# A recurrence and a token-mixing layer in one kernel: the same 1169 steps in another written order, with a fixed place for every tile

## The chip, the cores and the metric

The kernel runs on one core of one Trainium2 chip. The metric is the time of one execution on the device in microseconds (us); lower is better. A core has TensorE (PE, matmuls; its weight loads are shown apart as PEld), VectorE (DVE), ScalarE (ACT), GpSimd (POOL) and SyncE (SP, which issues the DMAs here). Each engine works through its own list of instructions strictly in order and waits on semaphores for the others.

## What is computed

The reference has two parts. The first is a gated linear recurrence over 768 positions for 4 batches of 8 heads of 48 values; its output is the input `x` of the second, a mixing layer:

```python
f = 1.0 / (1.0 + np.exp(-f_logit))
for t in range(S):
    state = f[:, :, t, :, None] * state + np.einsum('bhd,bhe->bhde', k[:, :, t], v[:, :, t])
    y[:, :, t] = np.einsum('bhd,bhde->bhe', q[:, :, t], state)
...
theta = x @ w_theta
zr, zi = x * np.cos(theta), x * np.sin(theta)
y = np.einsum('ts,bsd->btd', w_tok_r, zr) + np.einsum('ts,bsd->btd', w_tok_i, zi)
u = x + y
return u + np.maximum(u @ w_ch, 0.0)
```

The weights are 64-bit floats, which the kernel reads as pairs of 32-bit words and turns into 32-bit values on the chip.

## The kernel before

The 768 positions of a batch are six chunks of 128, so 24 chunks `m` in all. One function issues each step of the work for one chunk, one part of the weights or one group of outputs. The whole program is the table `ORDER`: 35 strings of two-letter step names. The loop at the end of the table's code calls the function of each name in turn, the n-th time for the n-th chunk, part or group. All five engines are under a manual schedule, so this one list fixes the order in which every engine does its instructions, the DMAs on SP's queue included. A suffix (`/A`, `/D`, `/P`) sets `here[0]`, and steps that ask for it (`on(...)`) go to ACT, DVE or POOL. Steps that name their engine ignore it.

The steps, by name:

- `lf lk lq lv lw` load the gates, keys, queries, values and one part of the weights.
- `gc go gs ge gp gq gk` clamp the gate's logits, take the log of the gate (ACT), sum it along the chunk (a scan on DVE), take both exponentials (ACT), keep the last column (POOL), and scale the queries and keys (`gk` is on DVE).
- `ke kt` transpose a chunk's keys on PE (tile `psk`) and copy them out (`ktok`). `sc` makes the scores (PE, `sk`), `up` the sums of the state (PE, also `sk`), `ma` masks the scores (DVE, `sc`). `sa st sm` update the state (`mid`, `st`). `qs` and `ou` make the chunk's output on PE (`py`), and `xc xt xs` copy it out (`x`), transpose it (PE, `pxt`) and keep it (`ut`).
- `th` multiplies by `w_theta` (PE, `pth`); `tn se ab tr` reduce the angle and take sine and cosine (DVE, ACT); `ro` multiplies by `x` (always on DVE); `zh zl` and `xh xl` split into a high and a low part.
- `d1 d2 d3 di d4 d5` decode and split the weights (`d2` is always on ACT).
- `f0 f1 f2` are the products with the token weights for one third of the channels (PE, `pm`); `v` adds them to `ut` (DVE); `uh ul` split the sum; `c` is the product with `w_ch` (PE, `pch`); `cv` finishes (DVE) and `so` stores.
- `fl` and `rv` find out whether a gate was too small for this way of computing. The branch that recomputes everything in that case is not taken here.

Batch 0 multiplies 32-bit values without a split (`pm<-value`, `pth<-value`); the other three use the split parts (`pm<-wp`). PE has three kinds of matmul: those with 128x128 weights and 384 columns; transposes with 128x128 weights and 128 columns; and the small ones of `sc up qs ou`, whose weights stand in 64 rows.

Tiles come from pools by a tag with a number of buffers, taken in turn: four PSUM banks `b`, two PSUM pairs `a`, six tiles `z`, 25 `wp`, three each of `f k q v x`. A tile waits for the last reader of the one that had its buffer before.

Of the kernel before, what the change touches and what calls it, by code (L numbers as in the profile page):

```python
# [49 lines left out]

ORDER = (
# [35 lines left out]
)  # L89


# [1 line left out]
def gla_moe_kernel(  # L93
# [16 lines left out]
    sb = ctx.enter_context(tc.tile_pool(name="sb", bufs=1))  # L110
    dram = ctx.enter_context(tc.tile_pool(name="dram", bufs=1, space=bass.MemoryType.DRAM))
    ps = ctx.enter_context(tc.tile_pool(name="ps", bufs=1, space=bass.MemoryType.PSUM))

    xt_d = dram.tile([B, DM, S], F32, tag="xt_d", name="xt_d")

# [465 lines left out]
    def recurrence(b):  # L581
# [6 lines left out]
        for p in range(NP):  # L588
# [3 lines left out]
                nc.sync.dma_start(t.rearrange("r (c t) -> r c t", c=NC), src[b, :, :, p, :].rearrange("c r t -> r c t"))  # L592
            nc.sync.dma_start(vr, vt[b, p])
            nc.scalar.activation(fr, fr, AF.Sigmoid)
            acc = [ps.tile([P, TH], F32, tag="b", bufs=4, name=f"acc{p}{h}") for h in range(NTH)]
            for e in range(D):

                sel = sb.tile([P, 2, 64], F32, tag="w", bufs=2, name=f"sel{p}{e}")
                for j in range(2):
                    nc.vector.tensor_copy(sel[:, j, :], ident[:, 64 * j + e:64 * j + e + 1].to_broadcast([P, 64]))  # L600
                kv = kvs[e % 2]
                for h in range(NTH):
                    hs = slice(h * TH, (h + 1) * TH)
                    bc = bank([P, TH], f"bc{p}{e}{h}")
                    nc.tensor.matmul(bc, sel.rearrange("p j m -> p (j m)"), vr[:, hs], start=True, stop=True)
                    nc.vector.tensor_tensor(kv[:, hs], kr[:, hs], bc, op=ALU.mult)
                nc.vector.tensor_tensor_scan(st, fr, kv, 0.0, ALU.mult, ALU.add)
                nc.vector.tensor_tensor(kv, qr, st, op=ALU.mult)
                for h in range(NTH):
                    nc.tensor.matmul(acc[h], pick[:, 47 - e:47 - e + P], kv[:, h * TH:(h + 1) * TH],  # L610
                                     start=(e == 0), stop=(e == D - 1))
# [5 lines left out]
    with tc.If(over[0] > 0, preferred_fallthrough_block=False):  # L617
        with tc.For_i(0, B, 1) as b:
            recurrence(b)
            for m in range(NC):  # L620
                if m == 0:
                    uts[0] = u_tile("r")
                uts[1] = uts[LAST]
                nc.sync.dma_start(u_slice(m), xt_d[b, :, m * C:(m + 1) * C].rearrange("(k p) t -> p k t", p=P))
                px = bank([P, DM], f"rpx{m}")
# [73 lines left out]
```

## Time and profile before

| | |
|---|---|
| median of 3 runs | 339.72 us (339.62 to 339.76) |
| the profiled execution's own time | 340.03 us |
| its span, from the first to the last instruction | 338.3 us |
| PE busy | 320.4 us, 95% of the span |
| DVE, ACT, POOL busy | 251.6, 188.7, 108.6 us |
| DMA | 45.54 MB |

The profiled execution took 1.73 us more than its span, and 0.31 us more than the median. "Busy" for PE is modelled from pipelined matmuls, so 95% doesn't say that 95% of PE's time was well used. Where PE is read closely, the starts of its instructions and the reasons for its waits count.

### The profile page before, as it was taken

What the parts mean: (1) busy time and instruction counts of PE and PEld (TensorE: products, weight loads), DVE (VectorE), ACT (ScalarE), POOL (GpSimd) and SP (SyncE); (2) the same over time, 40 slices, a digit from 0 to 9 for tenths busy, and PEclk for the clock granted to TensorE, in tenths of its full rate; (3) what the DMA queues carried; (4) which work ended last, traced back from release to release, by engine and by line L of the source; (5) the groups of instructions that cost most, each with busy time, mean ns of one, the idle gap of its engine ahead of it and who ended that gap; (6) DMA issues with size and microseconds to landing.
All of it is one profiled execution on the core that took longest, in us unless ns stands there. A gap on an engine that the chain in (4) does not pass through costs nothing. (4 is left out here: it accounts for less than half of the span.)

```text
span 338.3 us, 9998 instructions
## 1 busy us (share of the span) xinstructions
PE 320.4 (95%) x4320; PEld 283.2 (84%) x4320; DVE 251.6 (74%) x411; ACT 188.7 (56%) x308; POOL 108.6 (32%) x105
## 2 busy tenths in 40 slices
PE   0789999999999999999999999999999999999993
PEld 0676766776776789999999999999999999999992
DVE  5989999999999998898987857855437848534211
ACT  6787997995866755588476685244076114400010
POOL 3585152134418235701445423323212201300010
PEclk9999999999999999999999999999999999999998
DMA  7994994738761262374124320532121120000012
GB/s 256 382 401 168 317 372 151 249 114 323 244 224 30 64 230 82 91 233 141 33 85 149 122 79 2 187 114 84 40 73 48 47 73 27 0 2 0 11 60 78
DMA packets 21618, 45.54 MB, mean 135 GB/s; under 512 B 2368, under 2 KB 5440, under 8 KB 21568
## 3 DMA queue, kind: packets, MB, share of 16 engines
q1 hardware_dynamic: 21568, 44.84, 38.5%
q8 instruction: 36, 0.59, 0.7%
q14 instruction: 14, 0.11, 0.1%
HBM read 40.11 MB, written 4.72 MB: 133 GB/s over the span
## 5 line engine op out<-in xcount | busy, mean ns | idle before, releaser
L458 PE MATMUL pm<-wp,z 128*128 128x384 f32 x648 | 118.4, 337 | 0.0
L458 PEld LDWEIGHTS pm<-wp,z 128*128 128x128 f32 x648 | 112.4, 188 | 0.4
L458 PE MATMUL pm<-value,z 128*128 128x384 f32 x144 | 49.3, 487 | 0.0
L476 PE MATMUL pch<-uhl,wch 128*128 128x384 f32 x216 | 40.0, 337 | 0.0
L458 PEld LDWEIGHTS pm<-value,z 128*128 128x128 f32 x144 | 26.4, 190 | 15.2
L476 PEld LDWEIGHTS pch<-uhl,wch 128*128 128x128 f32 x216 | 37.4, 188 | 0.0
L469 POOL TENSOR_TENSOR uhl<-ut,uhl 128x384 fp32r<-128x384 f32 x13 | 14.2, 1094 | 67.0 <-ACT uhl L143 35.5
L236 POOL TENSOR_SCALAR f<-f 128x512 f32<-128x512 f32 x16 | 26.6, 1666 | 13.3 <-DMA f<-in_f_dram 12.5
L246 DVE TENSOR_TENSOR_SCAN f<-carry,f 128x512 f32<-128x512 f32 x24 | 29.8, 1246 | 1.4 <-ACT f L242 1.4
L257 POOL COPY pes<-p 128x4 f32<-128x4 f32 x24 | 10.5, 439 | 52.9 <-ACT p L253 52.9
L490 DVE SCALAR_TENSOR_TENSOR ut<-pch,ut 128x384 f32<-128x384 f32 x24 | 13.1, 550 | 18.8 <-PE pch L476 17.1
L308 PE MATMUL psk<-ident,k 128*128 128x128 f32 x96 | 16.9, 303 | 10.0 <-DVE k L266 10.0
L261 POOL TENSOR_TENSOR q<-q,p 128x512 f32<-128x512 f32 x12 | 17.3, 1446 | 23.1 <-ACT p L253 14.6
L462 DVE TENSOR_TENSOR ut<-pm,ut 128x384 f32<-128x384 f32 x24 | 13.0, 551 | 14.2 <-PE pm L458 14.2
L253 ACT ACTIVATE p<-f 128x512 f32<-128x512 f32 x24 | 15.1, 630 | 14.4 <-DVE f L246 6.8
L402 PE MATMUL pth<-wth,xh 128*128 128x384 f32 x108 | 23.0, 348 | 0.0
L308 PEld LDWEIGHTS psk<-ident,k 128*128 128x128 f32 x96 | 12.2, 153 | 12.3 <-issue 10.3
L435 DVE TENSOR_TENSOR w<-w,x 128x768 f32<-128x768 f32 x18 | 17.2, 962 | 6.3 <-ACT w L426 6.3
L143 ACT COPY x<-py 128x384 f32<-128x384 f32 x19 | 9.1, 478 | 22.5 <-PE py L361 22.1
L361 PEld LDWEIGHTS py<-v,sc 64*64 64x64 f32 x768 | 15.0, 140 | 7.4 <-issue 4.5
L143 ACT CAST uhl<-ut 128x384 fp32r<-128x384 f32 x7 | 3.6, 513 | 31.1 <-DVE ut L462 17.5
L266 DVE SCALAR_TENSOR_TENSOR k<-f,k 128x512 f32<-128x512 f32 x24 | 18.2, 758 | 1.8 <-ACT f L254 1.1
(83 smaller groups left out, 622.6 us busy)
## 6 DMA issues: line engine op xcount, KB each, us to landing
v<-in_v_dram SPq DMA_DIRECT2D x24, 384.0 KB, 4.3
f<-in_f_dram SPq DMA_DIRECT2D x24, 256.0 KB, 3.8
q<-in_q_dram SPq DMA_DIRECT2D x24, 256.0 KB, 4.1
k<-in_k_dram SPq DMA_DIRECT2D x24, 256.0 KB, 4.3
raw<-in_w_r_dram SPq DMA_DIRECT2D x12, 384.0 KB, 5.9
raw<-in_w_i_dram SPq DMA_DIRECT2D x12, 384.0 KB, 6.3
out_dram<-ut SPq DMA_DIRECT2D x21, 192.0 KB, 1.9
raw<-in_w_theta_dram SPq DMA_DIRECT2D x3, 384.0 KB, 6.4
```

Source lines behind the costliest of these rows:

```text
L236: on(nc.vector).tensor_scalar(ft, ft, F_MIN, None, op0=ALU.max)
L246: nc.vector.tensor_tensor_scan(fl, carry[:, pairs(h)].rearrange("p n t -> p (n t)"), fl, 0.0, ALU.mult, ALU.add)
L253: nc.scalar.activation(ps_[m][:, pairs(h)], ft, AF.Exp, scale=-1.0)
L261: on(nc.vector).tensor_tensor(qt, qt, ps_[m][:, pairs(h)], op=ALU.mult)
L266: nc.vector.scalar_tensor_tensor(kt, loaded["f", m][:, pairs(h)], E_TOP, kt, op0=ALU.min, op1=ALU.mult)
L308: nc.tensor.transpose(psks[m][:, p, :], loaded["k", m][:, p, :], ident)
L361: nc.tensor.matmul(out[HALF[t], j, p, :], scs[m][HALF[a], j, p, :], v2[HALF[a], t, p, :], start=(t == 0 and m % NC == 0 and p == 0), stop= ...
L402: nc.tensor.matmul(pths[m], l, r, start=(n == 0), stop=(n == len(ms) - 1))
L435: nc.vector.tensor_tensor(zs[m] if full else w, w, xs[m].unsqueeze(1).to_broadcast([P, 2, DM]), op=ALU.mult)
L458: nc.tensor.matmul(pms[g, d], l, r, start=(s == 0 and i == 0), stop=(s == NC - 1 and i == len(ms) - 1))
L469: on(nc.vector).tensor_tensor(us[g, d][:, 0], uts[g][:, d, :], us[g, d][:, 1], op=ALU.subtract)
L476: nc.tensor.matmul(pcs[g, d], l, r, start=(es[0] == 0 and n == 0), stop=(es[-1] == KD - 1 and n == len(ms) - 1))
```

## The change

The counts of all steps stay. `ORDER` is replaced as a whole. The suffixes change with it: clamps on POOL 16 to 18, scalings of queries on POOL 12 to 18, casts of `uh` on DVE 17 to 7, on ACT 7 to 17, and some others by one to six. The new table also writes `ro/P` 14 times and `d2/P` 8 times, and these two steps name their engines in the code. A table `PLACES` gives each tile its buffer by a digit. The pools are wrapped so that each buffer is a tag of its own. Its strings for `f k q v x w sd uhl` are plain rotations, as before; those for the banks `a` and `b`, for `z` and for the end of `wp` are not.

```diff
+PLACES = {
+    "a": "0110101100110101010101010101010101010101010101010",
...
 ORDER = (
-    "lf gc lf gc go go gs lf gc/P lq lk lv gs ge gq gp go ge gk lw lk gs ke kt up gp sc lq gq/P d1 lw lq d2 gk ke",
...
+    "lf lf gc gc go go lf gc/P gs lk ge gp lq gq/P lw gs gk ke d1 lv lk lq lf go sc ge kt/D up lk gs gk gp sa st",
...
+    class Placed:
+        def __init__(self, pool):
+            self.pool, self.made = pool, {}
+
+        def tile(self, shape, dtype, tag=None, bufs=1, name=None, place=None):
+            n = self.made[tag] = self.made.get(tag, -1) + 1
+            own = PLACES.get(tag, "")
+            if place is None:
+                place = int(own[n], 36) if n < len(own) else n % bufs
+            return self.pool.tile(shape, dtype, tag=f"{tag}{place}", bufs=1, name=name)
+
+    sb, ps = Placed(sb), Placed(ps)
```

Three places show how instructions move. A name's first number is the chunk or part (`psk3` is of chunk 3), and the line numbers of the changed kernel are 31 higher for the same code.

PE before, around the first product with `w_theta` (`pth0`), from the state sums of chunk 2 on:

```order
L322 MATMUL sk1_291<-v2_214,ktok2_250 64x48 x16
L371 MATMUL pxt0_361<-ident_70,x0_277 128x128 x3
L361 MATMUL py1_310<-v1_205,sc1_367 64x48 x16
L308 MATMUL psk3_398<-ident_70,k3_252 128x128 x4
L353 MATMUL py2_411<-st1_275,q2_180 64x48 x2
...
L402 MATMUL pth0_436<-value0_176,ut0_365 128x384 x2
L402 MATMUL pth0_436<-value1_198,ut0_365 128x384
L297 MATMUL sk2_446<-q2_180,k2_209 64x64 x16
L322 MATMUL sk2_446<-v3_396,ktok3_403 64x48 x16
L371 MATMUL pxt1_479<-ident_70,x1_405 128x128 x3
```

PE of the change, from the same state sums on:

```order
L353 MATMUL sk1_282<-v2_210,ktok2_276 64x48 x16
L384 MATMUL py1_326<-st0_184,q1_132 64x48 x2
...
L402 MATMUL pxt0_348<-ident_70,x0_317 128x128 x3
L339 MATMUL psk3_354<-ident_70,k3_244 128x128 x4
L433 MATMUL pth0_377<-value0_126,ut0_369 128x384 x2
L433 MATMUL pth0_377<-value1_271,ut0_369 128x384
L392 MATMUL py1_326<-v1_186,sc1_382 64x48 x16
L384 MATMUL py2_415<-st1_278,q2_190 64x48 x2
...
L328 MATMUL sk2_437<-q2_190,k2_177 64x64 x16
L353 MATMUL sk2_437<-v3_400,ktok3_404 64x48 x16
L402 MATMUL pxt1_474<-ident_70,x1_408 128x128 x3
```

The output products of chunk 1 (`ou`, `py1<-v1,sc1`) and the queries against the state of chunk 2 (`qs`, `py2`) stood ahead of `pth0` and now stand behind it; `qs` of chunk 1 has gone behind the state sums of chunk 2.

DVE before, up to the mask of chunk 2 (`sc2`):

```order
L303 TENSOR_TENSOR sc1_367<-sk1_291,causal_75 128x512
L334 TENSOR_TENSOR st2_369<-sk1_291,mid2_359 128x192
L192 SCALAR_TENSOR_TENSOR raw2_279<-raw2_279 128x768
L193 SCALAR_TENSOR_TENSOR value2_355<-raw2_279 128x768
L246 SCALAR_TENSOR_TENSOR f4_241<-carry_67,f4_241 128x512
L217 TENSOR_TENSOR wth0_84<-value0_176,wth1_85 128x768
L182 TENSOR_SCALAR raw3_343<-raw3_343 128x768
L182 TENSOR_SCALAR raw4_347<-raw4_347 128x768
L338 TENSOR_TENSOR st2_369<-st2_369,pes_83 128x192
L246 SCALAR_TENSOR_TENSOR f5_308<-carry_67,f5_308 128x512
L266 SCALAR_TENSOR_TENSOR k4_352<-f4_241,k4_352 128x512
L303 TENSOR_TENSOR sc2_485<-sk2_446,causal_75 128x512
```

DVE of the change, up to the same mask:

```order
L361 TENSOR_TENSOR mid2_362<-sk1_282,st1_278 128x192
L174 COPY ut0_369<-pxt0_348 128x3x128
L365 TENSOR_TENSOR st2_371<-sk1_282,mid2_362 128x192
L277 SCALAR_TENSOR_TENSOR f4_196<-carry_67,f4_196 128x512
L277 SCALAR_TENSOR_TENSOR f5_251<-carry_67,f5_251 128x512
L334 TENSOR_TENSOR sc1_382<-sk1_282,causal_75 128x512
L213 TENSOR_SCALAR raw2_273<-raw2_273 128x768
L297 SCALAR_TENSOR_TENSOR k4_352<-f4_196,k4_352 128x512
L444 SCALAR_TENSOR_TENSOR w0_406<-w0_406,pth0_377 128x384
L174 CAST wth1_85<-value0_126 128x768
L213 TENSOR_SCALAR raw3_412<-raw3_412 128x768
L334 TENSOR_TENSOR sc2_492<-sk2_437,causal_75 128x512
```

The copy of chunk 0 out of its transpose (`ut0`) has come from ACT to DVE, the mask of chunk 1 (`sc1`) has gone behind two scans, and the decoding of weight part 2 (`value2`) has gone behind the mask of chunk 2.

DVE at the end of the program before (group 7 is the last):

```order
L469 TENSOR_TENSOR uhl70_4212<-ut7_3935,uhl70_4212 128x384
L490 SCALAR_TENSOR_TENSOR ut6_3272<-pch60_4259,ut6_3272 128x384
L490 SCALAR_TENSOR_TENSOR ut6_3272<-pch61_4269,ut6_3272 128x384
L490 SCALAR_TENSOR_TENSOR ut6_3272<-pch62_4308,ut6_3272 128x384
L462 TENSOR_TENSOR ut7_3935<-pm72_4215,ut7_3935 128x384
L565 TENSOR_LOAD flag_88
```

DVE at the end of the changed program:

```order
L493 TENSOR_TENSOR ut7_3912<-pm72_4179,ut7_3912 128x384
L521 SCALAR_TENSOR_TENSOR ut6_3237<-pch60_4274,ut6_3237 128x384
L521 SCALAR_TENSOR_TENSOR ut6_3237<-pch61_4306,ut6_3237 128x384
L521 SCALAR_TENSOR_TENSOR ut6_3237<-pch62_4319,ut6_3237 128x384
L174 CAST uhl72_4332<-ut7_3912 128x384
L500 TENSOR_TENSOR uhl71_4330<-ut7_3912,uhl71_4330 128x384
L500 TENSOR_TENSOR uhl72_4332<-ut7_3912,uhl72_4332 128x384
L596 TENSOR_LOAD flag_88
```

A cast and two subtractions for the last group now stand on DVE behind the three finishing steps of group 6; before, they were on ACT and POOL.

## Rows read from the trace of the kernel before

**Rows 1.** The page's head and its first part: busy time, share, instructions.
```profile
span 338.3 us, 9998 instructions
...
PE 320.4 (95%) x4320; PEld 283.2 (84%) x4320; DVE 251.6 (74%) x411; ACT 188.7 (56%) x308; POOL 108.6 (32%) x105
```

**Rows 2.** PE's longest wait over the span: us in total, times, longest.
```profile
PE psk L308 <- DVE k L266: 10.0, 2, 9.6
```

**Rows 3.** Stretches: us, PE, PEld, DVE, ACT, POOL, granted clock, DMA, GB/s.
```profile
20.00:30.00 10.00, 8.64 (x132) 6.26 (x125) 8.99 (x14) 8.54 (x15) 4.82 (x6) 1.00 0.89 340
...
50.00:60.00 10.00, 9.92 (x181) 6.41 (x183) 9.93 (x17) 7.43 (x11) 2.61 (x4) 1.00 0.46 152
...
290.00:300.00 10.00, 10.00 (x59) 10.00 (x58) 5.87 (x8) 3.39 (x6) 1.52 (x2) 1.00 0.00 0
```

**Rows 4.** PE in order of time, 21 to 36 us: start, duration, operation.
```profile
21.70 1.10 PE L322 MATMUL sk<-v,ktok 64*64 64x48 f32 x31 [1.05 <-issue]
22.73 0.90 PE L371 MATMUL pxt<-ident,x 128*128 128x128 f32 x3
23.94 1.14 PE L361 MATMUL py<-v,sc 64*64 64x48 f32 x32 [0.30 <-DVE sc L303]
25.01 1.11 PE L308 MATMUL psk<-ident,k 128*128 128x128 f32 x4
26.05 0.35 PE L353 MATMUL py<-st,q 48*64 48x48 f32 x2
...
27.09 4.19 PE L402 MATMUL pth<-value,ut 128*128 128x384 f32 x6
31.20 0.69 PE L297 MATMUL sk<-q,k 48*64 48x64 f32 x32
31.72 0.63 PE L322 MATMUL sk<-v,ktok 64*64 64x48 f32 x32
...
34.54 2.20 PE L402 MATMUL pth<-value,ut 128*128 128x384 f32 x6
```

**Rows 5.** PE's weight loads (PEld) where groups change, and two matmul groups.
```profile
32.56 0.47 PEld L308 LDWEIGHTS psk<-ident,k 128*128 128x128 f32 x4
33.19 0.59 PEld L361 LDWEIGHTS py<-v,sc 64*64 64x64 f32 x32 [0.17 <-DVE sc L303]
...
38.08 1.59 PEld L402 LDWEIGHTS pth<-value,ut 128*128 128x128 f32 x6
40.21 0.59 PEld L361 LDWEIGHTS py<-v,sc 64*64 64x64 f32 x32 [0.55 <-DVE w L413]
...
52.44 1.46 PE L458 MATMUL pm<-value,z 128*128 128x384 f32 x4
...
56.01 2.74 PE L458 MATMUL pm<-value,z 128*128 128x384 f32 x8
...
133.85 1.08 PEld L458 LDWEIGHTS pm<-wp,z 128*128 128x128 f32 x6
135.19 0.59 PEld L361 LDWEIGHTS py<-v,sc 64*64 64x64 f32 x32 [0.25 <-issue]
```

**Rows 6.** DVE at the mask of chunk 2, and its group of copies.
```profile
32.42 0.69 DVE L303 TENSOR_TENSOR sc<-sk,causal 128x512 f32<-128x512 f32 x1 [0.48 <-PE sk L322]
...
L143 DVE COPY ut<-pxt 128x384 f32<-128x384 f32 x7 | 3.8, 548 | 1.4 <-PE pxt L371 1.4
```

**Rows 7.** DVE and the last DMA in order of time, near the end.
```profile
308.55 0.34 DVE L143 CAST uhl<-ut 128x384 fp32r<-128x384 f32 x1
...
318.53 0.55 DVE L469 TENSOR_TENSOR uhl<-ut,uhl 128x384 fp32r<-128x384 f32 x1
...
331.63 1.67 DVE L490 SCALAR_TENSOR_TENSOR ut<-pch,ut 128x384 f32<-128x384 f32 x3 [3.08 <-PE pch L476]
333.43 0.39 SPq L650 DMA_DIRECT2D out_dram<-ut  x1
```

**Rows 8.** One decoding instruction, 0 to 30 us: shortest, median, longest, in ns.
```profile
L182 DVE TENSOR_SCALAR raw<-raw x5: 537/554/957, 10.6 to 28.4; 128x768 int32<-128x768 int32 x4, 128x384 int32<-128x384 int32 x1
```

More of the change, by code (lines that the diff above doesn't have):

```diff
@@ L46 @@
 CUT = 0
-ORDER = (
[35 rows of a table removed]
+PLACES = {
+    "a": "0110101100110101010101010101010101010101010101010",
+    "b": ("012301230123120232033303032313203300021021002312020222222012312102022000230122012100102101"
+        "0031213213212302302323302132013"),
+    "f": "012012012012012012012012",
+    "k": "012012012012012012012012",
+    "q": "012012012012012012012012",
+    "sd": "010101010101010101010101",
+    "st": "01010101010101010101",
+    "uhl": "01230123012301230123012301",
+    "ut": "01201201",
+    "v": "012012012012012012012012",
+    "w": "010101010101010101010101",
+    "wp": "0123456789abcdefghijklmno012347569ab",
+    "x": "012012012012012012012012",
+    "z": "0123450123401340340352401352401352401",
+}
+ORDER = (
[36 rows of a table added]
 )
@@ L594, in recurrence @@
             nc.scalar.activation(fr, fr, AF.Sigmoid)
-            acc = [ps.tile([P, TH], F32, tag="b", bufs=4, name=f"acc{p}{h}") for h in range(NTH)]
+            acc = [ps.tile([P, TH], F32, tag="b", bufs=4, name=f"acc{p}{h}", place=h) for h in range(NTH)]
             for e in range(D):
@@ L603, in recurrence @@
                     hs = slice(h * TH, (h + 1) * TH)
-                    bc = bank([P, TH], f"bc{p}{e}{h}")
+                    bc = ps.tile([P, TH], F32, tag="b", bufs=4, name=f"bc{p}{e}{h}", place=2 + h)
                     nc.tensor.matmul(bc, sel.rearrange("p j m -> p (j m)"), vr[:, hs], start=True, stop=True)
@@ L621, in gla_moe_kernel @@
                 if m == 0:
-                    uts[0] = u_tile("r")
+                    uts[0] = sb.tile([P, KD, TH], F32, tag="ut", bufs=3, name="utr", place=(int(PLACES["ut"][-1]) + 1) % 3)
                 uts[1] = uts[LAST]
```

69 rows, old and new, of the table ORDER are left out of this document.

## The prediction

> **What bounds the kernel now.** I read the page first, then PE's waits, the stretches, and PE's own rows in order of time. PE is busy for 320.4 of 338.3 us [rows 1]. Its only large wait is the one before its first matmul, 9.6 us, for the first scaled keys from DVE [rows 2]. After that the stretches show three phases. From 20 to 30 us PE does 132 matmuls in 8.64 us, with DVE and ACT about 90% busy [rows 3]. From 50 to 60 us PE and DVE are both full, 9.92 and 9.93 of 10 us. From 290 to 300 us PE is full by its weight loads too (10.00), one matmul of 384 columns every 0.17 us, while DVE works for 5.87 us. So the end is set by PE, and a change of order can help in three places only: before PE is full, at the switches between kinds of matmul, which cost PE time without a visible wait, and behind the last matmul.
>
> The granted clock reads 1.00 throughout [rows 3], yet PE is at the lower of its two levels, 1.2 GHz, until about 31 us: the six matmuls of the first angle product take 4.19 us, the six of the second 2.20 us [rows 4]. Groups of 32 small matmuls start 1.07 us apart at 23.94 and 0.52 us apart at 31.20. What PE did before the rise: it worked without a break from 23.94, small groups and transposes first, and it rose at the end of the first angle product.
>
> **The change, part by part.** The sum is made from one point on PE: the output products of chunk 2 (`ou`, the third one), which start at 33.19 before [rows 5]. Counted in both orders, exactly the same 21 groups, that one included, lie up to there. So the time after the change is the time before, plus the shift of this point, plus what switches, waits and the end cost differently behind it.
>
> *The shift of that point.* The transposes of chunk 0's output (`pxt0`) are the twelfth PE group in both; the eleven ahead of them are the same with two pairs exchanged. I hold their start at 22.73 [rows 4]. Exchanging the pairs puts key 0 ahead of query 0 on DVE, which could bring PE forward by one such instruction, some 0.6 us. Against it, the state sums now wait for a copy on DVE behind a decoding step. I take 0 between 0.6 earlier and 0.7 later. The 1.05 us stop inside the sums of chunk 2 names no engine [rows 4]; I leave it where it falls.
>
> Before, `ou` of chunk 1, the transposes of key 3 and `qs` of chunk 2 lie between 23.94 and 27.09. In the change only the transposes do. The copy `ut0` moves to DVE at 0.55 us [rows 6], so it is ready at 22.73 + 0.90 + 0.55 = 24.2. The transposes of key 3 take 1.04 (25.01 to 26.05), from 23.65 to 24.7. The angle product then starts at 24.7 instead of 27.09.
>
> It takes 27.09 to 31.20, 4.11 us, as before; then `ou` and `qs` follow at the higher level, 0.52 each, and then four groups that took 31.20 to 33.19, 1.99 us. The point comes at 24.7 + 4.11 + 1.04 + 1.99 = 31.85, 1.35 earlier. This is the early bound. The late bound is DVE: before, it was free for the mask of chunk 2 at 32.42 - 0.48 = 31.94 and waited for PE [rows 6]. The changed DVE has 35 instructions ahead of that mask instead of 33, of like kinds. If DVE comes there no earlier, the mask ends at 31.94 + 0.69 = 32.63 and the point stands at 32.7, 0.5 earlier. I take -1.2, near the early bound, since DVE waits less for PE when the sums it needs come sooner.
>
> *Switches behind the point.* When PE goes from 128-row to 64-row weights, the next load doesn't begin while the last matmul runs. The pauses between the end of one group's loads and the next load [rows 5] are 0.54 after an unsplit product (39.67 to 40.21), 0.26 after a split one (134.93 to 135.19) and 0.16 after transposes (33.03 to 33.19). From the first some 0.1 comes off, since matmuls of this kind come every 0.32 us anyway (2.74 less 1.46 for four) and one load is about 0.2. Counted behind the point, entries to small groups are 7, 11 and 8 before, and 5, 10 and 10 after. That is -2 x 0.43 - 0.26 + 2 x 0.16 = -0.8 us. Ways out of small groups are 27 and 26; no row prices one well, so I count nothing, which leaves perhaps 0.2 more.
>
> *The end.* Before, PE's last three groups of nine matmuls had their subtractions from POOL. Now the last product of group 7's first two thirds is followed by two groups for group 6, and behind the finishing steps of these DVE casts and subtracts (0.34 and 0.55 [rows 7]). From the end of the second group: finishing 0.56 (1.67 for three), cast 0.34, subtraction 0.55, and about 0.25 to reach each other, 1.7 in all; PE has one group of nine, 9 x 0.17 = 1.53 [rows 3], as cover. That adds 0.2. If the cover were gone it would be 1.7. What lies behind, from 331.63 over the last DMA at 333.43 to the end, stays. Three more small stores of group 6 go out late on SP, behind steps that DVE ended some 4 us earlier; I count nothing, at worst one issue, 0.4 us.
>
> *Work moved between engines.* Six more query scalings and two more clamps on POOL, ten casts from DVE to ACT: DVE gets lighter, but it isn't the bound late (5.87 of 10 [rows 3]), so this counts nothing there. `ro/P` and `d2/P` move nothing: DVE has all 24 rotations in both lists and ACT all 16 decoding steps. Fixed places take away no wait that PE shows; PE's waits past the start are one small group. They may add some where a bank is given out again sooner. For new waits of all kinds I put 0.3, between 0 and 2.
>
> Sum: -1.2 - 0.8 + 0.2 + 0.3 = -1.5 us. Span 338.3 - 1.5 = 336.8; the profiled execution's time 340.03 - 1.5 = 338.5; against the median, 0.31 lower, 338.2 us.
>
> **The rivals.**
>
> *The clock rises later: slower.* The angle product now starts 2.4 us sooner after PE's start, with a pause for the copy ahead of it. Small groups alone, unbroken from 23.94 to 27.09, did not lift the level before [rows 4]. If the product's six matmuls don't lift it either, the seven groups up to and including the point run at half speed. They cost 3.6 us more (31.85 + 0.5 less 28.8, done twice), and the second angle product up to 2.0 more: 338.2 + 3.6 to 5.6, 342 to 344. It decides as soon as 1.5 us of full-speed work falls on the lower level. For it speaks the pause; against it that the product itself is the same unbroken 4.1 us.
> The Trainium skill ("TensorE: Matmul & The Clock Gate", section "What's actually happening") says that the array starts throttled and sustained work releases it, and that the same kernel can be released at different points from run to run. By it the loss before the release is under 1% of a typical span and not worth fitting, so the sum would keep its other terms. No run here shows the spread; three times stand within 0.14 us.
>
> *DVE becomes the bound from 40 to 110 us: no change.* PE and DVE were both full there [rows 3]. If PE arrives 1.5 us early and DVE's work ahead of each product is not shorter, PE waits those 1.5 us back: 339.7. For it: no slack shows in 50 to 60 us. Against it: the early point is earlier because DVE does the copy, mask and scans in another order, and six of the query scalings leave DVE.
>
> *POOL slows DVE: slower.* One kind of decoding instruction takes 0.54 us at best and 0.96 at worst in the first 30 us [rows 8]. If that comes from POOL working beside it, eight more large POOL instructions cost DVE up to 8 x 0.4 = 3.2 us. If all of it fell where DVE feeds PE, the time would be 338.2 + 3.2 = 341.4, and it decides from four of the eight on. Few of the eight are early, which speaks against it.
> The Trainium skill ("GPSIMD Engine Reference", section "1. Specifications") says that the two engines share interfaces to the memory, with contention for DVE instructions of some kinds. The spread agrees, but no row shows POOL as its cause.
>
> *More than forecast: faster.* The earlier bounds for `pxt0` and the switches together, with no new wait, give -0.6 - 1.35 - 1.0 + 0.2 = -2.75, 337.0.
>
> **How the numbers follow.** About 0.2%, 0.7 us, is what can be told from no change. The forecast, faster by 0.7 to 2.5 us, gets 0.54; more than that 0.08; DVE as the bound 0.14; the clock 0.13; POOL or another late wait 0.11. So faster has 0.62, no change 0.14, slower 0.24. The time is 338.2, the forecast's own range 337.2 to 339.0. From 336.9 to 341.2 leaves out most of the clock's case and part of the best one, under 2 in 10.
>
> **What would show it.** Right: the first angle product starts near 24.7, the second takes 2.2 us, the third `ou` starts near 31.9, PE has no wait over 0.5 us past 35 us, and 25 entries to small groups remain behind the point. Wrong: six matmuls in over 4 us a second time; PE waiting for DVE between 40 and 110 us; the last three groups on PE apart by more than 0.5 us.

## The result: slower by 0.8%, where 0.4% faster was forecast

The changed kernel takes 341.75 us (median of 7 runs, 340.95 to 343.25) against 339.72 us for the kernel before (7 runs). The ratio is 1.0079, with a 95% interval of 1.006 to 1.0098. The profiled execution took 341.52 us, with a span of 339.8 us. All medians below are of fast runs, so one run of e9, of 533.93 us, stands outside of them.

The head of the page and its first part answer to [rows 1]; the row of the granted clock stands in the page's second part, one digit for each fortieth of the span. Its digits ahead of 21.7 us stand where the trace has no record of the clock yet.

```profile
span 339.8 us, 10038 instructions
...
PE 319.3 (94%) x4320; PEld 282.0 (83%) x4320; DVE 255.3 (75%) x398; ACT 198.2 (58%) x321; POOL 117.6 (35%) x111
...
PEclk9998999999999999999999999999999999999997
```

PE's busy time fell by 1.1 us and the span grew by 1.5 us, so PE stood still for longer. The early stretch went the way that was forecast, and somewhat further. PE in order of time, which answers to [rows 4]:

```profile
21.17 0.79 PE L402 MATMUL pxt<-ident,x 128*128 128x128 f32 x3
21.79 0.60 PE L339 MATMUL psk<-ident,k 128*128 128x128 f32 x4
24.33 3.41 PE L433 MATMUL pth<-value,ut 128*128 128x384 f32 x6 [1.94 <-DVE ut L174]
27.67 1.07 PE L392 MATMUL py<-v,sc 64*64 64x48 f32 x32
...
31.36 0.72 PE L392 MATMUL py<-v,sc 64*64 64x48 f32 x32
32.01 2.20 PE L433 MATMUL pth<-value,ut 128*128 128x384 f32 x6
...
37.33 0.71 PE L392 MATMUL py<-v,sc 64*64 64x48 f32 x32 [0.66 <-DVE sc L334]
```

The first angle product starts at 24.33 (forecast 24.7), the second takes 2.20, and the third `ou` starts at 31.36 (forecast 31.85 to 32.7, before 33.19). PE leads by 1.83 us there in this execution.

**Where the lead went.** To see it, each moment of PE is given the end that it could still reach: the time now, plus the work that PE still has. That work is counted from the starts of weight loads in the trace at their closest spacing (0.322 us for unsplit products, 0.173 for split ones, 0.100 for transposes, 0.015 for small ones), plus 0.41, 0.26 or 0.21 us for going into a small group from each of these and 0.17 for going out. So it is an estimate from the traces, good to some 0.1 us, and it comes from one execution of each kernel. While PE never waits, this reachable end stays where it is; each wait moves it later.

```
PE's work left                285 us   218 us   0      end of the span
(about this time)             (45)     (113)    (333)
before                        330.8    330.9    332.1  338.3
change                        328.8    330.9    333.2  339.8
```

At 45 us the change leads by 2.0 us. At 113 us the lead is gone. A finer count shows where: with 240 us of work left, at some 90 us, the ends are 330.7 before and 329.0 after the change, so nearly all of the loss lies between 90 and 113 us. Behind that it loses 2.3 us where the kernel before loses 1.2, and the end behind PE's last load takes 0.5 more. So -2.0 + 2.0 + 1.1 + 0.5 = +1.6, against +1.5 of the spans.

The stretch in which the lead goes, of the change and then of the kernel before (us, then busy time and count of PE, PEld, DVE, ACT, POOL, granted clock, DMA share, GB/s):

```profile
60.00:115.00 55.00, 53.96 (x663) 35.92 (x662) 53.18 (x76) 42.24 (x68) 28.12 (x24) 1.00 0.58 200
```

```profile
60.00:115.00 55.00, 54.86 (x732) 37.67 (x724) 54.22 (x80) 42.69 (x70) 22.66 (x20) 1.00 0.56 190
```

DVE is nearly full in both. In the change it gets through 76 instructions of 0.70 us where it had 80 of 0.68, and POOL works 5.5 us more beside it. The part of it in which the lead goes, of the change and then of the kernel before:

```profile
90.00:113.00 23.00, 21.96 (x280) 14.28 (x281) 22.86 (x32) 16.02 (x26) 11.99 (x10) 1.00 0.47 164
```

```profile
90.00:113.00 23.00, 22.86 (x306) 15.47 (x305) 22.73 (x35) 16.56 (x27) 11.64 (x9) 1.00 0.46 155
```

DVE works without a wait there, and PE stops three times for it: 1.05 us until 94.15, 0.74 until 105.32 and 0.40 until 112.87, counted as above. Two of the three starts, and the last wait of DVE ahead of them:

```profile
83.74 0.69 DVE L297 SCALAR_TENSOR_TENSOR k<-f,k 128x512 f32<-128x512 f32 x1 [1.42 <-DMA k<-in_k_dram]
...
94.18 1.28 PE L433 MATMUL pth<-wth,xh 128*128 128x384 f32 x6 [0.59 <-DVE ut L493]
...
105.33 0.66 PE L339 MATMUL psk<-ident,k 128*128 128x128 f32 x4 [0.26 <-DVE w L444]
```

One place on DVE and POOL shows instructions of DVE that are stretched, in order of time:

```profile
101.52 1.65 POOL L292 TENSOR_TENSOR q<-q,p 128x512 f32<-128x512 f32 x1 [5.01 <-DMA q<-in_q_dram]
101.95 1.44 DVE L213 TENSOR_SCALAR raw<-raw 128x384 int32<-128x384 int32 x1
...
103.14 2.53 POOL L500 TENSOR_TENSOR uhl<-ut,uhl 128x384 fp32r<-128x384 f32 x2
103.31 1.49 DVE L297 SCALAR_TENSOR_TENSOR k<-f,k 128x512 f32<-128x512 f32 x1
104.73 0.54 DVE L444 SCALAR_TENSOR_TENSOR w<-w,pth 128x384 f32<-128x384 f32 x1
```

The key scaling takes 1.49 us beside POOL's subtractions; at 34.87 in the same trace, with POOL at rest, it takes 0.69. Not every overlap costs that: at 77.30 the same scaling stands beside one of POOL's subtractions from start to end and takes 0.68, while POOL's subtraction takes 1.56 (1.20 on the mean). The transposes of the key of 103.31 stood still on PE for 0.74 us until 105.33, and their row names the last step shown (`w<-w,pth`), which DVE did behind the scaling and which reads one of the four banks.

Behind 125 us there are two waits that the kernel before hasn't. ACT's copy of chunk 12 and SP's queue, in order of time:

```profile
157.31 0.38 SPq L525 DMA_DIRECT2D out_dram<-ut  x1
```

```profile
161.88 0.48 ACT L174 COPY ut<-pxt 128x384 f32<-128x384 f32 x1 [4.51 <-PE pm L489]
162.39 0.51 ACT L174 CAST xh<-ut 128x384 fp32r<-128x384 f32 x1
```

The row puts the 4.51 us down to PE, but the transposes that the copy reads ended at 158.7. The copy writes into the place of `ut` that group 1 had, so it has to wait for the stores of that group too; the last one was issued at 157.31, behind a load of values. By the trace it landed at 161.78, and the copy started at 161.88. PE's angle product of chunk 12 started 0.41 us late for it, at 162.96. The other wait, 0.37 us at 274.79, is of the scores of chunk 23 for a PSUM pair.

The end itself went as planned: PE's last 45 matmuls run without a gap.

```profile
325.71 7.96 PE L507 MATMUL pch<-uhl,wch 128*128 128x384 f32 x45
...
334.40 0.39 SPq L681 DMA_DIRECT2D out_dram<-ut  x1
```

The last DMA is issued 0.97 us later than before [rows 7], and 5.4 us pass behind it instead of 4.9. That half microsecond lies behind the last issue, in no instruction of the kernel; 0.2 of it is the last store itself, which lands 3.9 us after its issue instead of 3.7.

### The profile page after: what moved, and what is told of

The parts are those of the page before. It is cut to its first block, busy times and chain, and to the rows that moved or that the text cites. A ratio compares the mean times of both kernels' runs of the same rounds, so it can differ in the third digit from the quotient of the medians.

```text
span 339.8 us, 10038 instructions
## 1 busy us (share of the span) xinstructions
PE 319.3 (94%) x4320; PEld 282.0 (83%) x4320; DVE 255.3 (75%) x398; ACT 198.2 (58%) x321; POOL 117.6 (35%) x111
## 4 chain that ended last, share of the span: by engine, by line
PE 64%; DVE 2%; ACT 0%; issue 0%; DVEq 0%
PE pm L489 34%; PE pch L507 11%; PE pth L433 7%; PE py L392 3%; PE sk L328 2%; PE pxt L402 2%; PE py L384 2%; PE psk L339 2%; PE sk L353 2%; DVE wp L248 0%; DVE f L277 0%; DVE ut L521 0%; DVE k L297 0%; DVE sc L334 0%; ACT xh L174 0%
## 5 line engine op out<-in xcount | busy, mean ns | idle before, releaser
L267 POOL TENSOR_SCALAR f<-f 128x512 f32<-128x512 f32 x18 | 32.0, 1779 | 30.6 <-DMA f<-in_f_dram 28.1
L292 POOL TENSOR_TENSOR q<-q,p 128x512 f32<-128x512 f32 x18 | 26.8, 1489 | 37.3 <-ACT p L284 24.6
L174 ACT CAST uhl<-ut 128x384 fp32r<-128x384 f32 x17 | 8.6, 507 | 36.0 <-DVE ut L493 27.2
L500 POOL TENSOR_TENSOR uhl<-ut,uhl 128x384 fp32r<-128x384 f32 x13 | 15.4, 1192 | 40.4 <-ACT uhl L174 33.3
L297 DVE SCALAR_TENSOR_TENSOR k<-f,k 128x512 f32<-128x512 f32 x24 | 20.7, 863 | 6.2 <-ACT f L285 3.7
L424 POOL TENSOR_TENSOR xl<-ut,xh 128x384 fp32r<-128x384 f32 x8 | 9.6, 1200 | 37.6 <-ACT xh L174 28.0
L288 POOL COPY pes<-p 128x4 f32<-128x4 f32 x24 | 9.3, 388 | 38.3 <-ACT p L284 38.3
L466 DVE TENSOR_TENSOR w<-w,x 128x768 f32<-128x768 f32 x18 | 19.8, 1103 | 2.9 <-ACT w L457 2.9
```

The lines of the kernel that those rows point to most:

```text
L267: on(nc.vector).tensor_scalar(ft, ft, F_MIN, None, op0=ALU.max)
L292: on(nc.vector).tensor_tensor(qt, qt, ps_[m][:, pairs(h)], op=ALU.mult)
L297: nc.vector.scalar_tensor_tensor(kt, loaded["f", m][:, pairs(h)], E_TOP, kt, op0=ALU.min, op1=ALU.mult)
L466: nc.vector.tensor_tensor(zs[m] if full else w, w, xs[m].unsqueeze(1).to_broadcast([P, 2, DM]), op=ALU.mult)
L500: on(nc.vector).tensor_tensor(us[g, d][:, 0], uts[g][:, d, :], us[g, d][:, 1], op=ALU.subtract)
```

## The experiments

Theory A: POOL's larger share slows DVE where DVE is full, and PE waits for DVE. Theory B: single steps stand too late in the new order. Theory C, in the expectations of e1 to e4: the fixed places make PE wait for banks. Theory D (the prediction's rival): DVE sets the pace up to some 110 us whatever PE's lead, so the lead can't be kept. The reachable ends are from one profiled execution each, the times from five runs or more. Each ratio is to the kernel before as it ran beside that experiment (medians of 339.0 to 339.9 us).

**Parts of the change.** e1 has the new order and places with the engines of before; e2 the old order with the new engines; e3 the new order up to the third `ou` and the old one, with its engines, behind it; e4 the new order and engines. e2, e3 and e4 have no fixed places.

```diff
 e1: each step of the new ORDER with the suffix that it had before   (gk ke kt/D -> gk ke kt, ...)
 e2: each step of the old ORDER with the suffix that it has now
 e3: ... ma ou | the other steps in the old order with the old suffixes
 e4: PLACES = {} and no Placed(...)
```

e1: 

> The changed order and places, with every step on the engine that it had before (the same suffix for the same step and number). Theory A, that the extra POOL work slows DVE where DVE feeds PE: the early gain stays and most of the later waits go, 338 to 339.5 us, and the DVE instructions that were stretched (scaling of keys, rotation) come back near 0.76 and 0.96 us. Theory B, that the order itself puts DVE's work in the wrong sequence for PE: still 341 to 342.5 us. Theory C, that the places make PE wait for banks: also 341 to 342.5, with the waits at the same groups as in the change.

e2: 

> The order and the pools of before, with the engines of the change. Theory A: 341 to 343 us, with PE waiting for DVE between 40 and 130 us. Theories B and C: 339.5 to 340.5, about as before, since POOL and ACT have idle time and DVE gets lighter.

e3: 

> The changed order up to and with the third output product (ou of chunk 2), then the remaining steps in the order and with the engines of before; pools of before. All theories: the early gain of 1.8 us on PE (the third ou at 31.4 in place of 33.2). If the later part can keep it: 337.9 to 338.5 us. If DVE is the bound from 40 to 120 us whatever the order, PE waits it back there: 339.5 to 340.

e4: 

> The changed order and engines with the pools of before, without fixed places. Theory C: the waits for banks go, 339 to 340.5 us. Theories A and B: as the change, 341 to 342.5 us.

Measured: e1 380.43 us, ratio 1.1204 (1.1144 to 1.1265); e2 371.15, 1.0896 (1.0842 to 1.095); e3 347.6, 1.0227 (1.0179 to 1.0274); e4 344.12, 1.0135 (1.0094 to 1.0176). No theory expected times like those of e1 and e2. Order and engines can't be taken apart: either alone costs over 30 us, in many waits of PE for DVE and the others. The longest from 31 to 335 us, of e1 and of e2:

```profile
PE pch L506 <- DVE uhl L499: 3.8, 1, 3.8
PE pxt L401 <- DVE ut L173: 3.8, 1, 3.8
PE sk L352 <- DVE ktok L173: 2.5, 1, 2.5
```

```profile
PE psk L308 <- DVE k L266: 4.5, 5, 1.4
PE py L353 <- DVE x L143: 2.6, 3, 1.4
```

e3 reached the third `ou` at 32.34 and then has one wait of 5.9 us, for DVE, that ends at 38.97, so it says only that the early order leaves DVE with another rest of work. In e4 the time is 2.4 us above the change, so the fixed places are not what makes the change slow, and theory C falls.

**Less work on DVE: e5 (the change) and e6 (the kernel before).** Both leave the lowest three bits of the decoded weights out.

```diff
-        nc.vector.tensor_scalar(low, low, 29, None, op0=ALU.logical_shift_right)
-        nc.vector.scalar_tensor_tensor(low, high, 3, low, op0=ALU.logical_shift_left, op1=ALU.bitwise_or)
+        nc.vector.tensor_scalar(low, high, 3, None, op0=ALU.logical_shift_left)
```

e5: 

> The change without the step d1: DVE doesn't shift the low words, and the joining step takes the upper 20 bits of the fraction from the high word alone (the last 3 bits of each weight are left out). DVE has 16 instructions of about 0.65 us less, all before about 115 us, and 16 others get a cheaper form. Theory A, that the change is late because DVE (its work stretched by POOL) arrives late between 40 and 130 us: PE's waits past 35 us go, the point at the third ou stays, and the time is 337 to 339 us, below the same cut of before. Theory B, that the lost time lies in the order of PE's own groups or behind 130 us: 340.5 to 342.

e6: 

> The kernel before with the same cut (no d1, cheaper join). It shows no wait of PE past 31 us, so DVE's relief can only bring the start: 338.5 to 339.7 us by both theories. By theory A the change with this cut is 1 to 2 us faster than this kernel, by theory B 1 to 3 us slower.

Measured: e5 340.93, ratio to the full kernel before 1.0045 (1.0024 to 1.0065); e6 339.18, 0.9989 (0.997 to 1.0009). The stretch of e5, as above:

```profile
60.00:115.00 55.00, 54.67 (x673) 37.83 (x672) 47.18 (x67) 44.30 (x70) 27.33 (x24) 1.00 0.55 191
```

With DVE at 47 of 55 us PE gets 0.7 us of its loss back in this stretch. The reachable end moves from 327.4 to 328.1 over it, 0.7 instead of 2.1 (e6: 329.7 to 329.1). So most of the loss there hangs on DVE's work, as far as one execution of each shows. But e5's time is the one that theory B expected, not theory A: it still ends 1.7 us above e6, with a wait of 1.16 us at 161 us, the one for the store.

**Less work on POOL: e7 (the change) and e8 (the kernel before).** POOL's clamps work on 16 of 128 positions.

```diff
+        if here[0] is nc.gpsimd:
+            ft = ft[:, :, :16]
         on(nc.vector).tensor_scalar(ft, ft, F_MIN, None, op0=ALU.max)
```

e7: 

> The change with POOL's 18 clamps narrowed from 512 to 64 columns of a tile (the rest stays unclamped; no gate of these inputs is near the clamp). POOL has about 25 us less work. Theory A: the DVE instructions beside it are less stretched, and the clamped gate comes earlier, 339 to 340.5 us. Theory B: no change, 341 to 342.5.

e8: 

> The kernel before with POOL's 16 clamps narrowed in the same way. By both theories 339 to 340, since PE has no wait past 31 us that this could shorten; by theory A the change's loss against before shrinks from 2 us to under 1 between these two, by theory B it stays.

Measured: e7 343.43, ratio 1.0113 (1.0079 to 1.0147); e8 340.54, 1.003 (1.001 to 1.0051). Neither gains, and e8 is a little slower, for a reason that isn't known. The times of e7 speak against theory A, which expected 339 to 340.5. In its profiled execution, the slowest of its six, the clock fell back from 30.3 to 37.1 us, so the reachable end is late from the start (332.2 at 45 us); it still loses 2.0 us by 113 us, with 20.68 us of POOL's work from 60 to 115 us, less than the kernel before has (22.66).

**Steps moved ahead of waits: e9 and e10**, from theory B. The pieces of ORDER:

```diff
 e9 and e10:
-f0 f0 xh xl d4/D d4 f1 uh v tr        +f0 f0 v xh xl d4/D d4 f1 uh tr
-d3 d1 gk se lf                        +d3 gk se d1 lf
-gk xc/D qs                            +xc/D gk qs
-so so f1 ... lv sa gp so xc           +so so so f1 ... lv sa gp xc
-zl sc xt ul/P                         +zl xt sc ul/P
 e9 also:
-gs lf ma xs                           +ma gs lf xs
-gs tr ab/A ro lk                      +tr ab/A ro gs lk
-d5 xs/D th                            +xs/D d5 th
```

e9: 

> The change with eight steps moved by a few places, each ahead of a wait of PE that the changed trace shows: the mask of chunk 3 ahead of a scan (wait 0.73 us), one rotation ahead of a scan (0.34), the copy of chunk 5 ahead of a split of weights (0.29), a sum of group 0 ahead of a cast (1.05), a key scaling and an angle step ahead of a decoding step (0.74), a copy of x ahead of a key scaling (0.40), one store of group 1 issued earlier on SP (0.41), and a transpose ahead of scores near the end (0.37). Nothing is left out. If the loss behind the third `ou` is these single late steps, the sum of 4.3 us comes off and the time is 337.5, faster than before by some 0.6%. Rival: PE has no slack because DVE is full there, and each wait taken away comes back at the next step: less than 1.5 us comes off, 340.3 to 341.8.

e10: 

> Only five of those moves, the ones behind 90 us (waits of 1.05, 0.74, 0.40, 0.41 and 0.37 us). If single late steps make the loss: 3.0 us come off, 338.8. Rival (no slack on DVE): under 1 us comes off, 340.8 to 341.8.

Measured: e9 344.74 (median of five), ratio 1.0158 (1.0115 to 1.0201); e10 342.4, 1.0096 (1.0059 to 1.0134). So the moves brought nothing, and theory B isn't borne out for the stretch up to 115 us. Most of the waits that the moves aimed at are gone and larger ones stand elsewhere: in e9 PE starts 2.15 us late at 83 us, for a key, and 1.54 us late at 43 us, for a rotated tile; in e10 1.96 us at 97 us for a mask, behind which the clock fell as well (last section):

```profile
94.56 0.69 PE L432 MATMUL pth<-wth,xl 128*128 128x384 f32 x3
97.14 0.72 PE L391 MATMUL py<-v,sc 64*64 64x48 f32 x32 [1.88 <-DVE sc L333]
97.64 0.89 PE L327 MATMUL sk<-q,k 48*64 48x64 f32 x32
98.23 1.13 PE L352 MATMUL sk<-v,ktok 64*64 64x48 f32 x32
```

**More work on POOL: e11**, in the kernel before, on a spare tile.

```diff
         nc.vector.scalar_tensor_tensor(kt, loaded["f", m][:, pairs(h)], E_TOP, kt, op0=ALU.min, op1=ALU.mult)
+        if 4 <= m < 12:
+            for _ in range(4):
+                nc.gpsimd.tensor_tensor(spare, spare, spare, op=ALU.mult)
```

> The kernel before with 32 more POOL multiplications of 128x128 on a spare tile, four behind each key scaling of chunks 4 to 11, which feed nothing. It adds some 12 to 16 us of POOL work beside DVE, more than the 9 us that the change adds. If POOL beside DVE made the loss, DVE is stretched by some 8 us where it and PE are full, and the time is 342 to 344. If single late steps made it, POOL's extra work costs little: 339.7 to 340.5.

Measured: 344.17, ratio 1.0148 (1.0119 to 1.0177), about what theory A expected. Its stretch:

```profile
60.00:115.00 55.00, 52.68 (x758) 36.02 (x750) 54.45 (x76) 39.47 (x66) 36.11 (x37) 1.00 0.57 190
```

The 32 multiplications take 21.3 us of POOL and feed nothing. DVE has no wait for POOL from 45 to 115 us, so it is not that POOL's own results come late. DVE's mean instruction goes from 0.68 to 0.72 us, and the reachable end moves by 4.2 us where the kernel before loses 0.1.

**The late store and the key loads: e12, e13 and e14.** e12 has only the fourth and fifth move of e10. e13 adds two moves for keys whose loads DVE waits for in the change (0.89 us at 34 and 1.42 us at 82 us). e14 is e13 with the narrow clamps of e7.

```diff
 e13 and e14:
-lw d1 f1 ... lw lk sc       +lk lw d1 f1 ... lw sc        (the load of key 10)
-gk xt gs lf ma xs           +xt gs lf ma gk xs            (the scaling of key 5)
```

e12: 

> The change with two of the eight moves only: the last store of group 1 is issued on SP right behind the two before it, and the last transposes of chunk 21 stand ahead of the scores of chunk 23 on PE. With both moved (and three others), the waits of 0.41 and 0.37 us at 163 and 275 us were gone. If they stay away without the other three moves, PE's loss behind 125 us falls by 0.8 us and the time is 341.0. If they make no difference on the whole, 341.8.

e13: 

> The same two moves, and two for keys that DVE waits for in the changed trace (0.89 us at 34 us, 1.42 us at 82 us): the load of key 10 stands ahead of three weight loads on SP, and the scaling of key 5 behind a scan and a mask on DVE. If DVE, full from 31 to 115 us, loses the lead by these two waits for loads, DVE gets 2.3 us back, and PE with it: 339.0. Rival: the order has no slack anywhere, and the time comes back as other waits: 340.5 to 342.

e14: 

> The kernel of the run before with POOL's clamps narrowed to 16 of 128 positions of a pair (a part of the clamping left out), which takes about 7 us of POOL's work out of the stretch from 30 to 125 us, so that POOL has as much there as before the change. If POOL beside DVE is part of the loss at the rate that the extra POOL work showed in the kernel before (20 us more POOL, 5 us more time), it is 1.5 to 2 us faster than the run beside it: 337 to 337.5 if that run is at 339. If POOL has no part: within 0.5 us of the run beside it.

Measured: e12 343.48, ratio 1.0121 (1.0081 to 1.0161); e13 343.93, 1.0116 (1.0073 to 1.0159); e14 342.23, 1.009 (1.0054 to 1.0125). In e12 the copy of chunk 12 waits for its own transposes alone, and 2.2 us earlier:

```profile
159.68 0.48 ACT L173 COPY ut<-pxt 128x384 f32<-128x384 f32 x1 [1.37 <-PE pxt L401]
```

The reachable end moves by 1.3 us behind 113 us in e12, as before the change (1.2), instead of 2.3. So the two late waits (0.41 and 0.37 us) are most of the 1.1 us of that stretch. The whole time is no shorter, because this execution came late to the third `ou` (33.12). e12 also settles a rival for the stretch before: its DVE waits only 0.2 us for keys from 30 to 125 us, where the change's waits 2.3, and PE's reachable end still moves by 1.9 us from 45 to 113 us. So the late load of key 10 isn't needed for the loss. e13 got nothing: the later scaling of key 5 made PE wait 1.3 us for that key.

```profile
39.16 0.66 PE L338 MATMUL psk<-ident,k 128*128 128x128 f32 x4 [1.29 <-DVE k L296]
```

e14 has the same wait, but loses only 0.2 us from 45 to 113 us where e13 loses 2.3, and its median is 1.7 us below that of e13, what theory A had expected; the intervals of the two overlap, so neither the size nor the gain itself is certain. Its stretch and that of e13:

```profile
60.00:115.00 55.00, 54.98 (x667) 37.11 (x666) 54.44 (x78) 43.98 (x70) 22.14 (x24) 1.00 0.60 203
```

```profile
60.00:115.00 55.00, 54.21 (x627) 35.60 (x628) 54.51 (x76) 43.53 (x70) 24.96 (x22) 1.00 0.58 199
```

The reachable ends of the runs, by the same columns:

```
e4    328.2  331.3  333.7     e9    332.1  336.0  337.9
e5    327.4  328.1  331.2     e10   329.3  333.2  335.4
e6    329.7  329.1  330.3     e11   330.3  334.5  335.7
e7    332.2  334.2  337.2     e12   330.3  332.2  333.5
e8    331.5  331.0  332.6     e13   332.0  334.3  335.5
                              e14   331.3  331.5  333.2
```

Theory D is what the second column shows, in part. Whether PE starts the stretch at 328.2 (e4), 328.8 (the change), 330.8 (before), 331.3 (e14) or 331.5 (e8), it leaves it at 330.9 to 331.5. Less DVE work lowers this (328.1 and 329.1), work on POOL raises it (334.5). The others don't fit so plainly. e7 and e13 come to the stretch at 332 already and leave it at 334; e9 and e10, in which steps were moved, lose 3.9 us, part of it to waits that the moves made. e12 loses 1.9 and leaves at 332.2, and its trace names no cause beyond those of the change. The place of the loss isn't fixed either: in e4, e12 and e13 PE waits 1.1 us for a key at 79 to 82 us, where the change's own execution has no such wait. None of these versions beats the kernel before.

## Why the prediction was wrong

*The shift of the third `ou`: right, and somewhat larger.* Forecast -1.2, measured -1.83. It lay beyond the early bound because the first transposes came 1.56 us sooner than held (21.17 for 22.73; 0.9 of this is already there at the first matmul, 8.67 for 9.55), so that the angle product started when DVE had the copy ready, and because from the product's start to the next group it took 3.34 us instead of 4.11, its first part at the higher level. The two groups behind it gave 0.66 back, 1.70 us instead of 1.04, part of them at the lower level. DVE's list has 37 instructions ahead of the mask of chunk 2 where it had 36 (without clearings of tiles), not 35 and 33, and the late bound that hung on it didn't come to bear. That the size came out near the forecast is in part luck: e10 and e12 have the same steps up to there and reached the third `ou` at 31.91 and 33.12, and e11, which differs from the kernel before only by work on POOL from 28.8 us on, came there at 32.12 instead of 33.19, its clock having risen at 29.1 us. So the lead differs by more than a microsecond from one execution to the next.

*That the shift lasts: wrong.* This is the step that failed. The sum carried the shift from 33 us to the end, as if PE alone set the pace behind it. The rival "DVE becomes the bound from 40 to 110 us" came nearest for this stretch: both kernels leave it with the same reachable end, 330.9, and with less work on DVE (e5) the change loses 0.7 us there instead of 2.1. It was given a chance of 0.14. The row that it went by, PE and DVE both at 9.9 of 10 us from 50 to 60 us [rows 3], wasn't the place: from 45 to 75 us PE and DVE of the change are busy for 29.89 and 29.73 of 30 us, and the lead stays 2 us until about 90. It went where DVE worked without a wait and was late three times. What was said against the rival, that the early point comes earlier because DVE works in another order, holds for the early point only. Why DVE was late just there, by its order or by POOL beside it, no run separates; the wait for key 10 isn't needed for it (e12).

*Switches behind the point: right.* Forecast -0.8; the entries counted in the traces (5, 10 and 10 instead of 7, 11 and 8), priced by the costs of each kind above, make 11.31 instead of 12.16 us, -0.85. They are in the reachable ends already.

*New waits of all kinds: +0.3 forecast, +3.55 measured.* This is the term of the sum in which the failed step shows. Waits of PE behind the third `ou`, over 0.06 us each, sum to 7.6 us against 4.05. Some 2.4 us of it lie up to 120 us and are the lead given back to DVE (0.7 of them already at 37.33, for a mask, shown above); 1.1 us lie behind, 0.8 of them in the store's and the pair's wait. With the shift, the switches and the end this makes -1.83 - 0.85 + 3.55 + 0.5 = +1.4, against +1.5 of the spans. The "one issue, 0.4 us" that late stores might cost was looked for in group 6, at the end; it was a store of group 1, and it cost 0.41 to 1.16 us.

*The end: right on PE, 0.3 us off on the whole.* The groups of nine run on without a gap. The half microsecond behind the last DMA issue, which the forecast left as it was, came from no instruction.

*POOL slows DVE: it can; how much of the loss that is stays open.* e11 shows the mechanism at 4 to 5 us for 21 us of POOL, so 0.20 to 0.24 us for each; by this estimate the 5.5 us that POOL works more from 60 to 115 us would be 1.1 to 1.3 us of the 2.0 lost there. e14 agrees with it (22.14 us of POOL there, 0.2 us lost), but e7, with 20.68 us of POOL, lost 2.0 us all the same. So that POOL can slow DVE is shown, and the size of its part in the change is not. The Trainium skill ("GPSIMD Engine Reference", section "1. Specifications") says that POOL shares its memory interfaces with DVE, with contention for DVE instructions in a two-port mode or with two inputs from there. The trace agrees for the key scaling at 103.31, which has two (1.49 us for 0.69); at 77.30 the scaling kept 0.68 us, and POOL's instruction was the longer one. A decoding instruction with one input was stretched as well (1.44 us for 128x384 above, where 128x768 takes 0.54 at best [rows 8]); whether it ran in such a mode no row shows.

*The clock rises later: no, it rose sooner and fell back*, which no rival held (below). The second angle product ran at the higher level.

What stays open: the change's runs spread over 2.3 us and those of e12 and e13 over 3.5 and 3.8. First matmuls between 8.6 and 10.2 us, and the falls of the clock, both differ from one profiled execution to the next, but the times alone don't say which of them made a run slow.

## What to carry to other kernels

A lead won on one engine can be lost in any later stretch in which another engine has no slack; before an early gain is carried to the end, give that case a large share. Both engines at 99% don't say that it is lost there: here the lead outlived such a stretch and went in the next. Where two engines are full, moving single steps ahead of a wait can only move the wait (e9, e10), and the full engine's work is what to lower (e5). Before a lead is explained, look whether another execution has it. When a copy waits for an engine that had long been done, look for the store that still reads the place it writes to.

## What the runs showed of the hardware

The granted clock can fall again after it has risen, and in two places here did so behind a pause of PE of 2 us. In the change it is granted from 21.7 us; PE then stands still for 1.94 us ahead of 24.33, and from 25.1 to 28.5 us the level is half. Three stretches of the change (columns as above):

```profile
22.00:25.00 3.00, 1.06 (x6) 0.64 (x5) 3.00 (x6) 2.39 (x4) 1.17 (x1) 1.00 0.88 266
25.50:28.00 2.50, 2.50 (x16) 1.00 (x18) 2.50 (x5) 1.95 (x4) 2.37 (x1) 0.50 0.92 320
29.00:31.00 2.00, 1.84 (x85) 1.66 (x77) 1.21 (x3) 1.97 (x4) 1.46 (x1) 1.00 0.52 168
```

The same in the middle of e10, behind the wait of 1.88 us that ends at 97.14:

```profile
94.00:97.00 3.00, 1.26 (x8) 0.93 (x6) 3.00 (x4) 0.49 (x1) 2.07 (x2) 1.00 0.57 229
98.20:101.00 2.80, 2.80 (x81) 2.71 (x75) 2.80 (x5) 1.03 (x2) 0.00 (x0) 0.50 0.50 110
102.00:105.00 3.00, 3.00 (x11) 1.72 (x10) 2.89 (x5) 2.94 (x6) 2.17 (x2) 1.00 0.20 31
```

PE is busy throughout the middle stretch, at 1.2 GHz, and the 32 small matmuls at 98.23, shown above, last 1.13 us where they take 0.63 at the higher level [rows 4]. So a wait of 2 us can cost more than itself. It need not: in e9 the granted clock stays full from 29.6 to 343.7 us, over a pause of 1.66 us that makes PE start 2.15 us late.

```profile
83.29 0.66 PE L338 MATMUL psk<-ident,k 128*128 128x128 f32 x4 [1.66 <-DVE k L296]
```

The clock fell back at least once in ten of the fourteen experiments' profiled executions; in the kernel before it rose once, at 31.1 us, and stayed. The Trainium skill ("TensorE: Matmul & The Clock Gate", section "What's actually happening") says that the point of release differs from run to run and that the loss is under 1% of a span; here the first rise lies between 20.0 and 31.9 us over the runs, and by an estimate from that page's share, 1% of a span is 3.4 us, larger than the whole change, so that in this case it isn't small.
